# Attention in a fused block: P.V. runs that stop at the accumulator's copy, transposes of maxima joined to them, a sixth buffer of exponentials, and divisions forced behind a unit

## The chip, the cores and the metric

One NeuronCore of a Trainium2 chip runs the whole program. The metric is device time in microseconds (us) of one execution. TensorE is called PE here, VectorE DVE, ScalarE ACT, GpSimd POOL and the DMA-issuing SyncE SP, as in the profile.

## What is computed

A transformer block on 2048 tokens of 576 numbers: sliding-window attention (32 heads of 18, a window of 256 keys), and beside it a gated branch whose spatial product is a 2048 x 2048 matrix; both work on the same normed input.

```python
qkv = (x @ wqkv).reshape(B, S, 3, H, Dh).transpose(2, 0, 3, 1, 4)
scores = einsum("bhqd,bhkd->bhqk", q, k) * Dh ** -0.5
mask = (idx[:, None] - idx[None, :] >= 0) & (idx[:, None] - idx[None, :] < 256)
p = softmax(where(mask, scores, -1e9))
s = einsum("bhqk,bhkd->bhqd", p, v).transpose(...).reshape(B, S, D) @ wo
...
z = gelu(x @ w_in); z1 = z[:Fh]; z2 = layernorm(z[Fh:])
g = silu((z1 * (w_sp @ z2 + b_sp)) @ w_out)
return x_in + s * g
```

## The kernel before

The program goes through stages one after the other: projections to q, k, v and the second half of z (to 430 us of the profile), attention (442 to 892 us), the output projection `wo` (892 to 954 us), the spatial product (`acc`, to about 1655 us) and the last product (`c`). Only the order inside attention changes.

**Attention is cut into 16 units**: 4 heads times half of the tokens (1024 queries); units 0 to 7 have the first half, 8 to 15 the second. Of a unit PE does five kinds of work:

- *maxima* (M, L600): a score block with queries on the partitions, `sp`, 3 PSUM banks; DVE reduces it to a maximum per query (L604). 32 for a unit. When all are there, DVE makes the negative maxima (L613, L614), PE *transposes* them (T, L623), DVE copies them out (L626) and four DMAs put them into two extra rows of q (L630), so that the next product already has the maximum taken off.
- *scores* (S, L724): keys on the partitions, `tps`, 2 PSUM banks; ACT takes the exponential into a buffer `pt` (L728), one `pt` for four heads and one block of 128 keys, and POOL masks its two edges (L736, L739). `PTB` is the number of `pt` buffers, 5.
- *P.V.* (V, L752): four matmuls, one for each head and each of 32 columns, add one key block to up to 512 queries of the accumulator `ops`, of which there is one. A column of 128 queries of this, four heads together, is called a block below; the program has 360. When 512 queries are done, ACT copies the accumulator out (L767). The sums of the exponentials are in it as one more row.
- *fills* (L671): the first half of z, w_in's product for z1, which nothing in attention needs; 1944 matmuls of 512 columns in two streams, `ma` and `mb`, whose results ACT copies out (L676) and SP stores.

M, S and fills use 64 of the array's rows each, so that two streams run at once, one on each half of the rows; P.V. and T use all 128 rows. A change from the one to the other is called a switch here, and what stands between two of them a run or a region.

**After the second copy of a unit** `finish` queues the division: SP loads the sums (L814), DVE inverts them (L787), SP writes them out (L789) and reads them back four times, spread over partitions, into `rp` (L794, one buffer), POOL divides in four parts (L798), SP stores the result to `o_d` (L803). For the last unit the same is written after the loop (L810, L807, L808, L794, L798, L803).

**The order is written by a planner in the kernel**: it keeps a clock of its own with fixed costs, and emits at each step what its clock allows: a P.V. run if `pv_now` says so, else a score or a maximum, else a fill. `waiting` holds actions with a due time (loads, stores, divisions), which `tick` emits when the clock has passed it. All engines then execute in exactly the emitted order, each its own queue, SP's DMAs too. `GUARD` (150 ns) is the planner's margin for a finished operand. When nothing is left in the queues, the remaining `waiting` actions are emitted in order of time. Then follow 448 matmuls of `wo` (L1157), for 8 tiles of 256 tokens, two steps of 128 tokens each; each tile's operand is loaded from `o_d` (L978, L980), split by ACT (L1143) and DVE (L1144), and its result copied by ACT into one of two `so` buffers (L1190) that SP stores (L1192). Tiles 4 to 7 need the last unit.

Of the kernel before, what the change touches and what calls it, by code (L numbers as in the profile page):

```python
# [39 lines left out]
RMN = 16  # L40
QR = 5
STEPS = 27
GUARD = 150
# [6 lines left out]
DIVIDE_AT = (20000, 21200, 22400, 23600, 26500, 27000, 27500, 28000)  # L50
WARM = 54
SPB = 3
PTB = 5


ET = mybir.EngineType
# [8 lines left out]
def kernel(  # L65
# [170 lines left out]
    with ExitStack() as early:  # L236
# [283 lines left out]
        with ExitStack() as ph:  # L520
# [33 lines left out]
            waiting = []  # L554
            clock = 0.0
# [8 lines left out]
            def use(engine, ns, drain=0):  # L564

                busy[engine] = max(busy[engine], clock + 200) + ns
                return busy[engine] + drain

            def tick():
                for w in list(waiting):  # L570
                    if w[0] <= clock:
                        waiting.remove(w)
                        w[1]()
# [11 lines left out]
            maxima = {}  # L585
# [109 lines left out]
            def load_v(u):  # L695
# [3 lines left out]
                sp.dma_start(vg[:, :kn], v_d[k0:k0 + kn, :, g * 4 * VW:g * 4 * VW + 89].rearrange("s p c -> p s c"))  # L699
                vgs[u] = vg  # L700

            vgs, pts, left, o_ps, ous, last, todo, later = {}, {}, {}, {}, {}, [], [], []

            def steps_of(half):
# [37 lines left out]
            def pv(u, kb, qa, qz):  # L742
                g, half = UNITS[u]
                pt = pts[u, kb]
                k0 = 0 if half == 0 else 6
                c = qa // 4
                first = max(4 * c - 2, 0)
                if kb == first:
                    o_ps[c] = ops.tile([P, 512], F32, name="ops")
                hi = min(4 * c + 3, qz)  # L750
                for j in range(4):
                    pe.matmul(o_ps[c][32 * j:32 * j + 32, (qa - 4 * c) * P:(hi - 4 * c + 1) * P],  # L752
                              vgs[u][:, kb - k0, j * VW:j * VW + 32], pt[:, j, (qa - kb) * P:(hi - kb + 1) * P],
                              start=kb == first, stop=kb == 4 * c + 3, skip_group_check=True)
                spend_both((hi - qa + 1) * 218)
                if hi == qz:
                    pts.pop((u, kb))
                else:
                    later.append([0.0, u, kb, hi + 1, qz])
                if kb == 4 * c + 3:  # L760
                    if c % 2 == 0:
                        while parts.get(u - 2):
                            part(u - 2)
                        ous[u] = (ap_.tile([P, HS], F32, name="ou", bufs=2) if u < NU - 1 else
                                  tail()[:, 0:HS])
                    ou = ous[u]
                    act.activation(ou[:, c % 2 * 512:c % 2 * 512 + 512], o_ps.pop(c), AF.Copy)  # L767
                    free_at = use("act", 500, 120)
                    for t in later:
                        t[0] = free_at  # L770
                    if c % 2 == 1:
                        finish(u, ou)

            parts = {}

            def part(u):
                if parts[u]:
                    parts[u].pop(0)()

            def finish(u, ou):  # L780

                g, half = UNITS[u]
                cs = slice(half * HS, half * HS + HS)
                den = aa.tile([P, HS // 32], F32, name="den")
                rp = ap_.tile([P, HS], F32, name="rp", bufs=1) if u < NU - 1 else f32(slots[4][:, 0:HS])
                def invert():
                    dve.reciprocal(den, den)  # L787
                    t = use("dve", 270) - clock + 300
                    after(t + (1500 if u < NU - 2 else 300), lambda: sp.dma_start(r_d[u].rearrange("h (a b) -> (h a) b", b=HS // 32), den))  # L789
                    for i in range(4):  # L790
                        after(t + (FETCH_AT if u < NU - 2 else 4500) + 400 * i, partial(sums, i))

                def sums(i):
                    sp.dma_start(rp[32 * i:32 * i + 32, :], r_d[u][i:i + 1, :].to_broadcast([32, HS]))  # L794

                def divide(a, n=4):
                    hs = slice(a * HS // n, (a + 1) * HS // n)
                    pool.tensor_tensor(ou[:, hs], ou[:, hs], rp[:, hs], ALU.mult)  # L798
                    use("pool", 2900 / n)

                def store(i):
                    h = 4 * g + i
                    sp.dma_start(o_d[h * DH:(h + 1) * DH, cs], ou[32 * i:32 * i + DH, :])  # L803

                if u == NU - 1:
                    def put_last():
                        dve.reciprocal(den, den)  # L807
                        sp.dma_start(r_d[u].rearrange("h (a b) -> (h a) b", b=HS // 32), den)  # L808

                    last.extend([lambda: sp.dma_start(den, ou[DH::32, :]), put_last,  # L810
                                 lambda: [sums(i) for i in range(4)], lambda: [divide(a, 2) for a in range(2)],
                                 lambda: [store(i) for i in range(4)]])
                else:
                    after(busy["act"] - clock + 1000, lambda: sp.dma_start(den, ou[DH::32, :]))  # L814
                    sooner = 10000 if u == NU - 2 else 0
                    after(max(INVERT_AT - sooner, 4500), invert)
                    parts[u] = [partial(divide, a) for a in range(4)] + [partial(store, i) for i in range(4)]
                    for ns in DIVIDE_AT:
                        after(ns - sooner + (3500 if sooner else 0), partial(part, u))
# [183 lines left out]
            with ExitStack() as heads:  # L1003
# [41 lines left out]
                taken, max_done = {0: 2 * RMN}, {0: max_split(0)}  # L1045

                def pv_now():
                    n = next((i for i, t in enumerate(todo) if t[0] + GUARD > clock), len(todo))
                    if n >= 2 or (n and not score_queue[0] and not score_queue[1]):
                        size = sum(t[4] - t[3] + 1 for t in todo[:n])  # L1050
                        return n if size >= 9 or len(pts) >= PTB or not score_queue[0] else 0
                    return 0

                def pv_run(n):

                    spend_both(110)
                    for v in [v for v in maxima if taken.get(v) == 2 * RMN and max_done[v] <= clock]:
                        max_end(v)
                        ended.add(v)
                    for _ in range(n):  # L1060
                        pv(*todo.pop(0)[1:])
                        if later and later[0][0]:
                            todo[:0] = later
                            later.clear()
                            break
                    spend_both(220)

                while score_queue[0] or score_queue[1] or todo or filling:
# [3 lines left out]
                    while opened < NU and all(not q or q[0][0] >= opened for q in score_queue):  # L1072
                        open_unit(opened)
                        opened += 1
                    full = [v for v in maxima if taken.get(v) == 2 * RMN and max_done[v] + GUARD <= clock]
                    n = pv_now()
                    if n or full:
                        pv_run(n)
# [609 lines left out]
```

## Time and profile before

| | us |
|---|---|
| median of three runs | 1862.79 |
| the three runs | 1862.79, 1864.56, 1860.42 |
| the profiled execution | 1859.38 |
| its span, first to last instruction | 1857.3 |
| first score of attention | 442.05 |
| last P.V. run begins | 885.49 |
| first matmul of `wo` | 891.87 |

The profiled execution is 3.4 us below the median of the runs. Times in the profile are counted from the span's start. A timeline row gives start, duration, engine, source line, operation, output and inputs, and the count of merged instructions; in brackets stands the idle time of the engine before it and what ended it. A matmul's duration is its latency: consecutive ones overlap, so that the distance between starts tells what one costs. P.V. matmuls leave two records each (1408 for 704). Of the 512 maxima 468 have a record inside attention's window, the rest being missing or earlier.

### The profile page before, as it was taken

What the parts mean: (1) busy time and instruction counts of PE and PEld (TensorE: products, weight loads), DVE (VectorE), ACT (ScalarE), POOL (GpSimd) and SP (SyncE); (2) the same over time, 40 slices, a digit from 0 to 9 for tenths busy, and PEclk for the clock granted to TensorE, in tenths of its full rate; (3) what the DMA queues carried; (4) which work ended last, traced back from release to release, by engine and by line L of the source; (5) the groups of instructions that cost most, each with busy time, mean ns of one, the idle gap of its engine ahead of it and who ended that gap; (6) DMA issues with size and microseconds to landing.
All of it is one profiled execution on the core that took longest, in us unless ns stands there. A gap on an engine that the chain in (4) does not pass through costs nothing.

```text
span 1857.3 us, 38172 instructions
## 1 busy us (share of the span) xinstructions
PE 1823.3 (98%) x14363; PEld 1590.3 (86%) x14363; DVE 1138.2 (61%) x2289; ACT 947.8 (51%) x1758; POOL 430.7 (23%) x507
## 2 busy tenths in 40 slices
PE   8999999999999999999999999999999999999998
PEld 8999999997777777776898878888888888899998
DVE  6321333467766677771246788667876567758876
ACT  5433322225666576667467566465554544444443
POOL 3332333334465455556100000111100000000000
PEclk9999999999999999999999999999999999999999
DMA  8885688887566666754776777789777656786554
GB/s 254 206 229 169 232 278 281 290 258 224 154 194 168 187 174 179 189 161 142 239 266 225 236 239 244 258 293 302 252 262 234 185 183 198 250 266 187 160 159 134
DMA packets 266920, 405.75 MB, mean 218 GB/s; under 512 B 52336, under 2 KB 180592, under 8 KB 266608
## 3 DMA queue, kind: packets, MB, share of 16 engines
q1 hardware_dynamic: 266736, 403.32, 70.4%
q8 instruction: 113, 1.85, 0.4%
q14 instruction: 71, 0.58, 0.1%
HBM read 285.35 MB, written 117.09 MB: 217 GB/s over the span
## 4 chain that ended last, share of the span: by engine, by line
PE 82%; DVE 7%; DMA 5%; SPq 2%; ACT 2%; issue 2%; POOL 0%; DVEq 0%; ACTq 0%; POOLq 0%
PE acc L1431 34%; PE mb L206 11%; PE c L1522 7%; PE ma L671 6%; PE mb L671 5%; PE ma L206 5%; PE ops L752 4%; PE tps L724 3%; PE sp L600 3%; PE wops L1157 2%; SPq L363 1%; DMA st_d<-qkhl 1%; DVE junk L604 1%; DVE spl L116 1%; PE ma L380 0%
## 5 line engine op out<-in xcount | busy, mean ns | idle before, releaser
L1431 PE MATMUL acc<-spl,zh 128*128 128x512 f32 x1008 | 392.6, 390 | 1.1 <-DVE spl L116 0.9
L1431 PE MATMUL acc<-sph,zh 128*128 128x512 f32 x1008 | 392.2, 389 | 0.0
L1431 PE MATMUL acc<-sph,zl 128*128 128x512 f32 x1008 | 392.1, 389 | 0.0
L604 DVE CUSTOM_DVE_ANT_0 junk<-sp,band 128x384 bf16<-128x384 f32 (+1 forms) x512 | 276.4, 540 | 114.9 <-PE sp L600 33.6
L728 ACT ACTIVATE pt<-tps 128x384 f32<-128x384 f32 (+2 forms) x576 | 231.2, 441 | 121.6 <-PE tps L724 78.0
L116 DVE TENSOR_TENSOR spl<-spr,sph 128x1024 fp32r<-128x1024 f32 x168 | 210.2, 1251 | 40.0 <-ACT sph L115 39.3
L671 PE MATMUL mb<-b,z1wh 64*128 64x512 f32 x648 | 225.2, 400 | 2.5 <-ACT z1o L676 2.1
L671 PE MATMUL ma<-b,z1wh 64*128 64x512 f32 x648 | 224.8, 399 | 0.6 <-ACT zt L948 0.4
L1431 PEld LDWEIGHTS acc<-spl,zh 128*128 128x128 f32 x1008 | 189.2, 188 | 41.7 <-DVE spl L116 2.8
L1431 PEld LDWEIGHTS acc<-sph,zh 128*128 128x128 f32 x1008 | 189.3, 188 | 39.3
L1431 PEld LDWEIGHTS acc<-sph,zl 128*128 128x128 f32 x1008 | 189.3, 188 | 39.3
L115 ACT ACTIVATE zh<-b 128x384 fp32r<-128x384 f32 x168 | 87.3, 520 | 211.1 <-PE acc L1431 206.7
L115 ACT ACTIVATE sph<-spr 128x1024 fp32r<-128x1024 f32 x168 | 176.0, 1048 | 14.5 <-DMA spr<-in_w_sp_dram 5.3
L724 PE MATMUL tps<-att 56*128 56x384 f32 (+1 forms) x576 | 177.2, 345 | 2.2 <-ACT pt L728 1.2
L116 DVE TENSOR_TENSOR zl<-b,zh 128x384 fp32r<-128x384 f32 x168 | 99.6, 593 | 124.0 <-ACT zh L115 123.9
L600 PE MATMUL sp<-att 54*128 54x384 f32 (+1 forms) x512 | 161.2, 349 | 2.0 <-DVE mx L604 1.8
L1522 PE MATMUL c<-b,o 128*128 128x288 f32 x1056 | 143.3, 295 | 0.5 <-DVE o L116 0.5
L1522 PEld LDWEIGHTS c<-b,o 128*128 128x128 f32 x1056 | 141.0, 188 | 0.8 <-DVE o L116 0.7
L949 DVE BATCH_NORM_STATS2 st<-zt 128x6 f32<-128x384 f32 x96 | 49.3, 548 | 132.1 <-ACT zt L948 132.0
L671 PE MATMUL ma<-b,z1wl 64*128 64x512 f32 x324 | 128.4, 396 | 0.0
L671 PE MATMUL mb<-b,z1wl 64*128 64x512 f32 x324 | 127.8, 394 | 0.0
L724 PEld LDWEIGHTS tps<-att 56*128 56x128 f32 x576 | 99.7, 184 | 30.5 <-issue 9.5
(219 smaller groups left out, 4189.6 us busy)
## 6 DMA issues: line engine op xcount, KB each, us to landing
spr<-sc_d SPq DMA_DIRECT2D x96, 512.0 KB
spr<-in_w_sp_dram SPq DMA_DIRECT2D x72, 512.0 KB
zr<-z_d SPq DMA_DIRECT2D x144, 192.0 KB
z_d<-zt SPq DMA_DIRECT2D x48, 384.0 KB
z_d<-z1o SPq DMA_DIRECT2D x72, 256.0 KB
z1t<-z_d SPq DMA_DIRECT2D x72, 256.0 KB
y_d<-z1t SPq DMA_DIRECT2D x72, 256.0 KB
a<-in_w_sp_dram SPq DMA_DIRECT2D x64, 256.0 KB
```

The costliest lines, as they stand in the source:

```text
L115: act.activation(hi, src, AF.Copy)
L116: dve.tensor_tensor(lo, src, f32(hi), ALU.subtract)
L206: pe.matmul(banks[h][:, :n], *both[h][i], start=i == 0, stop=i == STEPS - 1)
L600: pe.matmul(ps[:, :w], q_of(u, j)[0:54, i * P:(i + 1) * P], k_of(u, j)[0:54, k0:k0 + w], start=True, stop=True)
L604: dve.tensor_tensor_reduce(out=junk[:, :w], in0=ps[:, :w], in1=band[:, m0:m0 + w], scale=1.0, scalar=-3.0e38, op0=ALU.add, op1=ALU.max, ac ...
L671: pe.matmul(ps, w, x_, start=n == 0, stop=n == STEPS - 1)
L724: pe.matmul(ps[:, :m * P], k_of(u, j)[:, (kb - base) * P:(kb - base + 1) * P], q_of(u, j)[:, (a - lo) * P:(a - lo + m) * P], start=True, s ...
L728: act.activation(pt[:, j, d0:d0 + n * P], ps[:, (qa - a) * P:(qa - a + n) * P], AF.Exp, scale=scale)
L752: pe.matmul(o_ps[c][32 * j:32 * j + 32, (qa - 4 * c) * P:(hi - 4 * c + 1) * P], vgs[u][:, kb - k0, j * VW:j * VW + 32], pt[:, j, (qa - kb) ...
L949: dve.bn_stats(st2[:, s, pc, :], zv)
L1431: pe.matmul(acc[j], z[:, ps], w[:, cs], start=s == i == 0 and n in OPENS, stop=s == 7 and i == 2, skip_group_check=True)
L1522: pe.matmul(banks[key][:, :288], y, w, start=begin and k == n == 0, stop=close and k == 8 and n == 2, skip_group_check=True)
```

## The change

Six edits, all in the planner:

1. `pv_run` also stops a run when the accumulator has been given to ACT's copy (`if not o_ps: break`), and `pv_now` allows no new run before that copy is done on the planner's clock (`ops_free`). Before, a run stopped at a copy only if key blocks were left over that also belong to the next 512 queries.
2. A P.V. run needs 12 blocks instead of 9 (unless buffers are full or no score is left).
3. A unit's maxima are transposed only 1000 ns (`LATE`) after the planner's end of their negation; and, apart from a P.V. run that happens anyway, only when the score queue's ninth entry (`DUE` = 8) belongs to that unit.
4. `PTB` is 6.
5. `finish` of a unit first emits what is left of the four divisions of the unit before.
6. `tick` goes through its actions in order of due time.

```diff
-PTB = 5
+LATE = 1000
+DUE = 8
+PTB = 6
...
-                for w in list(waiting):
+                for w in sorted(waiting, key=lambda w: w[0]):
...
+            ops_free = [0.0]
...
                     free_at = use("act", 500, 120)
+                    ops_free[0] = free_at
...
                 cs = slice(half * HS, half * HS + HS)
+                while len(parts.get(u - 1, ())) > 4:
+                    part(u - 1)
...
                 def pv_now():
+                    if not o_ps and ops_free[0] + GUARD > clock:
+                        return 0
...
-                        return n if size >= 9 or len(pts) >= PTB or not score_queue[0] else 0
+                        return n if size >= 12 or len(pts) >= PTB or not score_queue[0] else 0
...
+                def max_due(v):
+                    queue = score_queue[0]
+                    return not queue or queue[min(DUE, len(queue) - 1)][0] >= v
...
-                    for v in [v for v in maxima if taken.get(v) == 2 * RMN and max_done[v] <= clock]:
+                    for v in [v for v in maxima if taken.get(v) == 2 * RMN and max_done[v] + LATE <= clock]:
...
                             break
+                        if not o_ps:
+                            break
...
-                    full = [v for v in maxima if taken.get(v) == 2 * RMN and max_done[v] + GUARD <= clock]
+                    full = [v for v in maxima if taken.get(v) == 2 * RMN and max_done[v] + LATE <= clock
+                            and max_due(v)]
```

The number of instructions of each kind on PE stays the same: 704 P.V. matmuls, 576 scores, 512 maxima, 16 transposes, 1944 fills. What changes is how they stand:

| PE, attention | before | changed |
|---|---|---|
| runs of P.V. | 71 | 56 |
| transposes alone, between two regions | 12 | 7 |
| transposes at the head of a P.V. run | 4 | 9 |
| switches (stretches of full rows) | 83 | 63 |
| runs that go on behind an accumulator's copy | 4 | 0 |
| fills behind the last P.V. | 48 | 0 |

PE, the end of one unit and the begin of the next (units 11 and 12); `ops` is the accumulator, a new number is a new accumulator, `pt` the exponentials. Before:

```order
L724 MATMUL tps_13029<-att0_2227 128x384
L752 MATMUL ops_12825<-pt_12849,vg_12021 32x128 x4
L752 MATMUL ops_13039<-pt_12895,vg_12540 32x128 x4
L752 MATMUL ops_13039<-pt_12935,vg_12540 32x256 x4
L724 MATMUL tps_13050<-att0_2227 128x384
L600 MATMUL sp_13055<-att3_6847 128x384
```

and with the change, where the line numbers are 2 or 3 higher:

```order
L727 MATMUL tps_13104<-att0_2227 128x384
L755 MATMUL ops_12926<-pt_12852,vg_12075 32x256 x4
L755 MATMUL ops_12926<-pt_12908,vg_12075 32x128 x4
L602 MATMUL sp_13125<-att3_6847 128x384
L727 MATMUL tps_13129<-att0_2227 128x384
...
L625 MATMUL sp_13221<-ident_70,ms_13141 64x128
L755 MATMUL ops_13225<-pt_12974,vg_12607 32x128 x4
L755 MATMUL ops_13225<-pt_13016,vg_12607 32x256 x4
L755 MATMUL ops_13225<-pt_13056,vg_12607 32x384 x4
L755 MATMUL ops_13225<-pt_13103,vg_12607 32x384 x4
```

The run that went on from one accumulator into the next is cut at the copy, and the next accumulator's run comes 38 rows later, with four key blocks and a transpose (L625) at its head.

PE, the end of attention. Before, from the last run but one:

```order
L752 MATMUL ops_14676<-pt_14634,vg_14047 32x384 x4
L752 MATMUL ops_14676<-pt_14672,vg_14047 32x256 x4
L671 MATMUL ma_14747<-b0_92,z1wh_14254 128x512
L671 MATMUL mb_14732<-b0_92,z1wl_14255 128x512
L671 MATMUL ma_14747<-b3_95,z1wh_14254 128x512
L671 MATMUL mb_14732<-b0_92,z1wh_14254 128x512
L752 MATMUL ops_14676<-pt_14712,vg_14047 32x128 x4
L671 MATMUL ma_14747<-b0_92,z1wl_14255 128x512
...
```

and with the change, from the last score before the last three runs:

```order
L727 MATMUL tps_14757<-att0_2227 128x256
L755 MATMUL ops_14635<-pt_14590,vg_14152 32x256 x4
L755 MATMUL ops_14635<-pt_14631,vg_14152 32x128 x4
L727 MATMUL tps_14769<-att0_2227 128x256
L727 MATMUL tps_14772<-att1_2228 128x256
L755 MATMUL ops_14776<-pt_14590,vg_14152 32x128 x4
...
L755 MATMUL ops_14776<-pt_14739,vg_14152 32x256 x4
L727 MATMUL tps_14799<-att1_2228 128x256
L755 MATMUL ops_14776<-pt_14756,vg_14152 32x128 x4
L1172 MATMUL wops_14868<-att2_2229,ohl0_14855 128x288 x2
```

The last fill now stands eight rows ahead of the first of these, with seven scores between them, and `wo` comes right behind the last P.V., where 48 fills stood.

POOL, the same place, with the change (`pt_14756` is the last key block's exponentials, `ou_14405` the result of unit 14):

```order
L739 AFFINE_SELECT pt_14711<-pt_14711 128x4x128
L742 AFFINE_SELECT pt_14711<-pt_14711 128x4x128
L739 AFFINE_SELECT pt_14739<-pt_14739 128x4x128
L804 TENSOR_TENSOR ou_14405<-ou_14405,rp_14600 128x256 x3
L739 AFFINE_SELECT pt_14756<-pt_14756 128x4x128
L804 TENSOR_TENSOR ou_14405<-ou_14405,rp_14600 128x256
L804 TENSOR_TENSOR att5_14473<-att5_14473,att4_6849 128x512 x2
```

Three divisions of unit 14 stand ahead of the last mask; before, all four stood ahead of the last four masks. On SP the store of unit 14's result (L809) moves from ahead of the last fills' stores to the row just ahead of the load of the last unit's sums (L816).

## Prediction

> **What bounds the kernel now.** First the page, then the stretches of 25 us through attention.
>
> ```profile
> PE 1823.3 (98%) x14363; PEld 1590.3 (86%) x14363; DVE 1138.2 (61%) x2289; ACT 947.8 (51%) x1758; POOL 430.7 (23%) x507
> PE 82%; DVE 7%; DMA 5%; SPq 2%; ACT 2%; issue 2%; POOL 0%; DVEq 0%; ACTq 0%; POOLq 0%
> ```
>
> ```profile
> core 0: us, PE busy (x) PEld busy (x) DVE busy (x) ACT busy (x) POOL busy (x), PEclk, DMA share, GB/s
> 625.00:650.00 25.00, 23.06 (x196) 18.12 (x198) 16.46 (x59) 11.59 (x26) 8.85 (x15) 0.93 0.65 169
> 675.00:700.00 25.00, 25.00 (x271) 19.52 (x265) 18.10 (x64) 17.97 (x46) 14.91 (x23) 1.00 0.73 203
> 900.00:925.00 25.00, 23.65 (x176) 23.19 (x175) 7.46 (x7) 11.01 (x17) 3.61 (x2) 1.00 0.79 247
> ```
>
> PE carries 82% of the chain that ended last, and in attention it is covered nearly everywhere: 25.00 of 25 us in an ordinary stretch, with DVE and ACT at 18. But a busy PE here is latency laid end to end; what one switch, wait or fill costs is seen only between starts. So attention is bound by PE's in-order queue: fills, which wait for nothing, fill it up while scores and maxima wait for ACT and DVE.
>
> At the end something else binds:
>
> ```profile
> 885.49 0.43 PE L752 MATMUL ops<-pt,vg 128*32 128x128 f32 x8
> 891.55 0.39 PE L671 MATMUL ma<-b,z1wl 64*128 64x512 f32 x1
> 891.87 22.66 PE L1157 MATMUL wops<-att,ohl 128*128 128x288 f32 x168
> 915.40 0.78 PE L1157 MATMUL wops<-att,ohl 128*128 128x288 f32 x4 [0.87 <-ACT ohl L1143]
> 916.66 37.04 PE L1157 MATMUL wops<-att,ohl 128*128 128x288 f32 x276 [0.48 <-DVE ohl L1144]
> ```
>
> ```profile
> 885.99 0.60 ACT L767 ACTIVATE att<-ops 128x512 f32<-128x512 f32 x1 [1.91 <-PE ops L752]
> 888.00 0.62 SPq L810 DMA_DIRECT2D den<-att  x1
> 896.90 4.57 DMA att<-r_d
> 901.69 3.62 POOL att L798 x2
> 905.32 1.37 SPq L803 DMA_DIRECT2D o_d<-att  x4
> 910.56 2.90 DMA s_d<-so
> 914.09 1.27 ACT ohl L1143
> ```
>
> The chain of waits goes from the last unit's copy over its sums, their inverse, the division and its store (SP stands at L803 until POOL is done at 905.3); behind this in SP's queue is the store of `so`, for which ACT's queue stands before it can split the operand of the fourth token tile. PE reaches that tile with only 0.87 + 0.48 us to wait, and is then continuous for 37 us. So the time of everything behind is the last P.V. plus 916.66 - 885.49 = 31.2 us, whatever PE does meanwhile. **The question is when the last P.V. comes.** The 48 fills behind it merely fill that latency.
>
> **Switches: -6.6 us.** A run of eight blocks, and one of one block:
>
> ```profile
> 785.40 0.39 PE L671 MATMUL mb<-b,z1wh 64*128 64x512 f32 x1
> 785.72 1.93 PE L752 MATMUL ops<-pt,vg 128*32 128x384 f32 x24
> 787.58 0.44 PE L600 MATMUL sp<-att 54*128 54x384 f32 x1
> ...
> 459.22 0.38 PE L724 MATMUL tps<-att 56*128 56x256 f32 x1
> 459.53 0.43 PE L752 MATMUL ops<-pt,vg 128*32 128x128 f32 x8
> 459.89 0.44 PE L600 MATMUL sp<-att 54*128 54x384 f32 x1
> ```
>
> From the last start before to the first behind it is 2.18 us with eight blocks and 0.67 with one: 0.22 for a block, and 0.45 without any. In those 0.45 a half-array matmul would have run anyway: fills follow each other at 0.12 us (48 stand between 885.49 and 891.55 above, in some 5.7). That leaves 0.33 us for a switch, in both directions together. There are 83 before and 63 after: 20 x 0.33 = 6.6. The blocks, 360, stay.
>
> **Waits for the copy within a run: -3.7.** The four runs that went on behind a copy look like this:
>
> ```profile
> 664.14 0.33 PE L724 MATMUL tps<-att 56*128 56x384 f32 x1
> 664.41 0.86 PE L752 MATMUL ops<-pt,vg 128*32 128x256 f32 x16
> 666.03 0.43 PE L752 MATMUL ops<-pt,vg 128*32 128x128 f32 x8 [0.76 <-POOL ou L798]
> 666.38 0.50 PE L671 MATMUL ma<-b,z1wh 64*128 64x512 f32 x1
> ```
>
> Four blocks in 2.24 us where 0.45 + 4 x 0.22 = 1.33 would do: 0.91, and 4 x 0.91 = 3.7. The profile names POOL, but the releaser is ACT's copy between the two accumulators (L767 stands elsewhere as the releaser of L752). The change cuts all four runs there; scores, maxima and fills stand in the gap.
>
> **Transposes: -2.9.** They stood 150 ns of planner time behind DVE's negation, and DVE is later than planned:
>
> ```profile
> L623 PE MATMUL sp<-ident,ms 128*64 128x128 f32 x15 | 4.5, 299 | 2.9 <-DVE ms L614 2.9
> ```
>
> 2.9 us of idle PE. With 1000 ns, and a place in front of a P.V. run for 9 of 16, this should go. What is late next is q's two extra rows, which the unit's scores need: between a transpose and its unit's first score stand about as many PE instructions as before (in the first half a few more, in the second the same), so I put nothing there; the bound is the 0.7 us that L724 waits for `att<-mhl` now, doubled.
>
> **The fills that stood behind the last P.V.: +5.7.** They come before it now, 48 x 0.12. This takes back most of the switches: PE saves time, but spends it on fills that were hidden in the latency at the end.
>
> **An end without fills: +4.8.** From the last fill to the last P.V. PE now has only what ACT and POOL let it have:
>
> ```profile
> 877.28 1.51 ACT L728 ACTIVATE pt<-tps 128x384 f32<-128x384 f32 x3
> 880.90 0.66 ACT L728 ACTIVATE pt<-tps 128x256 f32<-128x256 f32 x2 [1.42 <-PE tps L724]
> 884.21 0.63 POOL L736 TENSOR_SCALAR_AFFINE_SELECT pt<-pt 128x512 f32<-128x512 f32 x1 [1.31 <-ACT pt L728]
> ```
>
> Eight scores, paced by two `tps` banks (score 0.34, exponential 0.5 or 0.38, two in flight: 0.35 to 0.45 each), and one split among them, 4.2 us; a P.V. run of three blocks 0.9; ACT's copy 0.6 and its hand-over 0.1; the next accumulator's run of eleven blocks 2.5; then the last score 0.35, its exponential 0.3, its mask 0.7, the last block 0.4: 10.0 us. PE's work in it is 15 blocks (3.3), eleven scores (0.9), three switches (1.0): 5.2. So 4.8 us of PE are lost. Bounds: 2.5, if the scores' exponentials have run ahead under the fills; 7, if the last mask is held up (below).
>
> **Smaller terms.** The load of the last unit's sums was issued 1.4 us behind the end of the copy (886.59 to 888.00), since SP issued two tiles' loads of `o_d` first; now those stand earlier, but four stores of unit 14 stand just ahead of it, 1.4 us of issue: -0.3, bounds -1.4 and +1. The 12-block rule, the sixth buffer and the sorted actions change the order only, and are in the counts. A stall at 640 us has no cause in the order alone:
>
> ```profile
> 633.32 7.21 DMA z_d<-z1o
> 641.28 0.49 PE L671 MATMUL mb<-b,z1wh 64*128 64x512 f32 x1 [1.54 <-ACT z1o L676]
> 643.16 0.62 PE L671 MATMUL mb<-b,z1wl 64*128 64x512 f32 x1
> 640.00:645.00 5.00, 3.72 (x20) 3.36 (x22) 2.54 (x10) 3.96 (x10) 2.00 (x3) 0.72 0.64 177
> ```
>
> A store of a fill's result took 7.2 us, ACT's copy waited for its buffer, PE for ACT, 1.54 us; then the granted clock was 0.72 over 5 us (1.4 us lost, fills at 0.62 instead of 0.39). Where SP's queue is interleaved otherwise this may go or stay, 0 to -2.9; I take -1.5. The same dip can come in the new idle time at the end: with `wo` right behind the last P.V., PE waits for copy and split of the first tile (0.60 + 1.26 + 1.23, by ACT and DVE behind 885.99) and later some 3.5 us at the fourth tile. The first is covered by the chain; behind the second PE is what binds. 0 to 1.4 by the row above; +0.7.
>
> [...]
>
> **Sum.** -6.6 - 3.7 - 2.9 + 5.7 + 4.8 - 0.3 - 1.5 + 0.7 = -3.8 us. On the profiled 1859.4 that is 1855.6; the runs' median lies 3.4 above that execution, and 1862.8 - 3.8 = 1859.0. About 0.2%, 3.7 us, is what a measurement of this kernel can tell from no change; the forecast stands on that line.
>
> **Rivals.**
>
> *No gain*: the freed PE time is all spent on the end. Fills (5.7), the empty end at its bound (7) and the dip (1.4) are 14.1 against 13.2 from switches, copies and transposes: 1863.7, give or take 1.5. For it: the end is bound by latency, not by PE. Against: 7 needs the mask held up too.
>
> *Slower: the restart behind longer runs.* During P.V., ACT has two `tps` banks to work off, 0.5 us each (877.28: three in 1.51), then stands still; now runs of four key blocks, some 2.5 us, are the common ones. The time in which ACT stands is the same P.V. time less 1.0 us for each of 71 runs before, and for each of 56 now: 15 us more of it in all. Had ACT no slack, attention would be 15 longer and the time 1862.8 - 3.8 + 15 = 1874. It has (17.97 of 25 us busy above), but in the last two units fills are few. From half of these 15 on the change is slower by 0.2%; a little over that, 1868, is its likeliest size.
>
> *The mask behind the divisions* belongs with it in sign: POOL's last mask stands behind three divisions of unit 14, which need the reread sums.
>
> ```profile
> 857.05 0.60 ACT L767 ACTIVATE ou<-ops 128x512 f32<-128x512 f32 x1 [0.98 <-PE ops L752]
> 874.63 1.42 POOL L798 TENSOR_TENSOR ou<-ou,rp 128x256 f32<-128x256 f32 x2 [1.00 <-DMA rp<-r_d]
> ```
>
> Now it is 17.0 us from the copy's end to the first division. The order gives about 8 us of PE work from unit 14's last P.V. to the last fill, and 9 to the last mask: 17. Three divisions are 2.2 us, so that the last P.V. would be late by about as much: 1861.2, in the second bound above.
>
> *More than forecast*: the end loses only 2.5, the load of sums comes right behind the copy (-1.4), the stall at 640 us is gone whole (-2.9), no dip: -3.8 - 2.3 - 1.1 - 1.4 - 0.7 = -9.3, 1853.5.
>
> *The change doesn't do what it says*: the order shows that it does; no chance.
>
> **How the numbers follow.** Forecast, 0.48, 1856 to 1862 by itself, a little over half of it beyond the line (0.27); no gain, the mask's 1861.2 included, 0.18; slower 0.16; more than forecast 0.18. Faster by over 0.2%: 0.27 + 0.18 = 0.45; within: 0.21 + 0.18 = 0.39; slower: 0.16. The range reaches from the large gain to the edge of the slower case, 1853 to 1866.5, and leaves out most of that one and the tail of the gain.
>
> **What would show it.** Right: L767 no longer a releaser of L752 on PE; L623's wait for L614 near 0; 63 switches at 0.33; the last P.V. between 880 and 884 us, and `wo`'s long group 31 us behind it, with 3 us of idle PE ahead of it. Wrong: a wait of L752 for POOL L804 at the last block (divisions), idle PE between scores with L731 as releaser through units 8 to 15 (restart), or the last P.V. later than 886 us.

## Result and the profile after

| | before | changed |
|---|---|---|
| median of the runs shown together, us | 1862.63 | 1905.85 |
| the four runs | 1860.42 to 1864.56 | 1902.45 to 1909.69 |
| ratio (95% interval) | | 1.0232 (1.0207 to 1.0257) |
| profiled execution; its span | 1859.38; 1857.3 | 1905.45; 1903.6 |
| last P.V. run begins | 885.49 | 932.50 |

The change costs 43 us; the forecast was 1859.0. All of it is lost in attention: the span grew by 46.3 us, the last P.V. comes 47.0 later. Two lines of the changed kernel's page, engine shares and the chain that ended last:

```profile
PE 1844.1 (97%) x14363; PEld 1611.2 (85%) x14363; DVE 1138.4 (60%) x2289; ACT 949.5 (50%) x1758; POOL 429.2 (23%) x507
PE 78%; DMA 9%; DVE 6%; SPq 3%; ACT 2%; issue 2%; POOL 1%; DVEq 0%; ACTq 0%; POOLq 0%
```

PE is busy for 21 us more with the same 14363 instructions, and carries less of the chain; DMA has 9% instead of 5. One row for attention, from the first score to the last P.V., shows what the longer time is made of (columns: stretch, its length, busy time of PE, PEld, DVE, ACT, POOL, granted clock, DMA share, GB/s). Before, then changed:

```profile
442.00:885.50 443.50, 431.82 (x4272) 328.52 (x4273) 281.60 (x1001) 295.72 (x729) 237.36 (x350) 1.00 0.63 174
```

```profile
443.90:932.50 488.60, 455.29 (x4309) 350.33 (x4310) 278.52 (x999) 298.42 (x731) 234.48 (x348) 0.95 0.58 159
```

Of the 45.1 us, 21.6 are idle PE (443.50 - 431.82 = 11.7 before, 488.60 - 455.29 = 33.3 now) and 23.5 are longer busy time. Of the latter the 48 fills that moved ahead of the last P.V. are 5.7 at the price of the prediction. The other 17.8 fit the clock: in the trace's clock records PE runs at 0.50 for 44.4 us of this stretch, 3.4 before, and half of the 41.0 more would be 20.5. **Nearly half is waiting, and most of the rest is the clock behind the waiting.** The largest stall, on PE, and the clock around it:

```profile
548.22 0.39 PE L673 MATMUL ma<-b,z1wl 64*128 64x512 f32 x1
554.24 0.68 PE L727 MATMUL tps<-att 56*128 56x384 f32 x1 [5.63 <-ACT pt L731]
```

```profile
546.00:552.00 6.00, 1.75 (x12) 0.94 (x11) 1.96 (x8) 0.00 (x0) 3.03 (x4) 0.99 0.70 194
552.00:558.00 6.00, 3.76 (x20) 3.76 (x22) 1.40 (x5) 3.16 (x8) 1.53 (x3) 0.50 0.26 84
558.00:564.00 6.00, 6.00 (x67) 4.71 (x66) 3.04 (x11) 3.33 (x10) 1.93 (x3) 0.94 0.49 117
```

PE stands for 5.63 us for an exponential; when it goes on, the granted clock is 0.50 and the matmuls take 0.62 instead of 0.39. The exponential is late because ACT stands at a copy of the accumulator:

```profile
543.61 0.56 ACT L688 ACTIVATE z1wh<-z1raw 128x384 fp32r<-128x384 f32 x1
553.21 0.60 ACT L770 ACTIVATE ou<-ops 128x512 f32<-128x512 f32 x1 [9.05 <-DMA z_d<-z1o]
```

The profile names a store of a fill's result, which this copy has nothing to do with. Its output `ou` has two buffers, so unit 3 writes where unit 1's result is still being stored; SP and POOL show that store and its division:

```profile
543.61 0.27 SPq L809 DMA_DIRECT2D o_d<-ou  x1
...
549.19 0.31 SPq L809 DMA_DIRECT2D o_d<-ou  x1
```

```profile
540.77 2.81 POOL L804 TENSOR_TENSOR ou<-ou,rp 128x256 f32<-128x256 f32 x4 [4.25 <-DMA rp<-r_d]
```

POOL waited 4.25 us for the reread inverses, SP for POOL, ACT for the stores. There used to be more time. Unit 1's second copy, then before the change that copy, the unit's last store, and unit 3's first copy:

```profile
516.15 0.60 ACT L770 ACTIVATE ou<-ops 128x512 f32<-128x512 f32 x1 [0.92 <-PE ops L755]
```

```profile
502.65 0.60 ACT L767 ACTIVATE ou<-ops 128x512 f32<-128x512 f32 x1 [0.91 <-PE ops L752]
...
534.69 0.32 SPq L803 DMA_DIRECT2D o_d<-ou  x1
...
541.47 0.60 ACT L767 ACTIVATE ou<-ops 128x512 f32<-128x512 f32 x1
```

The last store is issued some 33 us behind the second copy in both (549.19 - 516.15 = 33.0 now, 32.0 before). But ACT reaches the copy of the unit after next 28.0 us behind it now (553.21 - 9.05 = 544.16), where 38.8 us lay between before. The second stall of this kind came about otherwise, on the side of the store: unit 4's copy is reached 38.9 us behind unit 2's, but unit 2's last store is issued 40.2 us behind, since POOL begins the unit's divisions 30.0 us behind its copy instead of 22.0.

```profile
576.73 0.33 SPq L809 DMA_DIRECT2D o_d<-ou  x1
581.52 0.60 ACT L770 ACTIVATE ou<-ops 128x512 f32<-128x512 f32 x1 [6.04 <-DMA o_d<-ou]
```

The other family of stalls is on DVE. Its queue, and SP's, at PE's stall of 3.8 us at 824:

```profile
821.39 0.28 DVE L628 COPY mhl<-sp 64x128 f32<-64x128 f32 x1
827.28 0.35 DVE L793 RECIPROCAL den<-den 128x32 f32<-128x32 f32 x1 [5.62 <-DMA den<-ou]
827.55 0.50 DVE L606 CUSTOM_DVE_ANT_0 junk<-sp,band 128x384 bf16<-128x384 f32 x1
```

```profile
818.71 0.47 SPq L642 DMA_DIRECT2D z1raw<-in_w_z_dram  x1
820.23 0.28 SPq L809 DMA_DIRECT2D o_d<-ou  x1
...
821.85 0.62 SPq L820 DMA_DIRECT2D den<-ou  x1
```

The load of the sums was issued behind a weight of 576 KB and the stores of the unit before; the reciprocal stands 5.62 us for it, the next maximum (L606) stands behind the reciprocal, and PE waits for a free `sp` bank. Over the program, from the waits of the changed kernel (us in total, times, longest):

```profile
DVE den L793 <- DMA den<-ou: 23.5, 9, 5.6
...
PE tps L727 <- ACT pt L731: 14.6, 9, 5.6
...
PE sp L602 <- DVE mx L606: 9.7, 9, 3.8
...
ACT ou L770 <- DMA o_d<-ou: 6.0, 1, 6.0
```

### The profile page after: what moved, and what is told of

The parts are those of the page before. It is cut to its first block, busy times and chain, and to the rows that moved or that the text cites. A ratio compares the mean times of both kernels' runs of the same rounds, so it can differ in the third digit from the quotient of the medians.

```text
span 1903.6 us, 38155 instructions
## 1 busy us (share of the span) xinstructions
PE 1844.1 (97%) x14363; PEld 1611.2 (85%) x14363; DVE 1138.4 (60%) x2289; ACT 949.5 (50%) x1758; POOL 429.2 (23%) x507
## 4 chain that ended last, share of the span: by engine, by line
PE 78%; DMA 9%; DVE 6%; SPq 3%; ACT 2%; issue 2%; POOL 1%; DVEq 0%; ACTq 0%; POOLq 0%
PE acc L1446 34%; PE mb L208 10%; PE c L1537 7%; PE ma L208 6%; PE ma L673 5%; PE mb L673 5%; PE ops L755 4%; PE tps L727 2%; PE sp L602 2%; PE wops L1172 2%; SPq L365 1%; DMA den<-ou 1%; DMA att<-st_d 1%; DMA st_d<-qkhl 1%; DVE junk L606 1%
## 5 line engine op out<-in xcount | busy, mean ns | idle before, releaser
L606 DVE CUSTOM_DVE_ANT_0 junk<-sp,band 128x384 bf16<-128x384 f32 (+1 forms) x512 | 275.8, 539 | 143.9 <-PE sp L602 55.4
L673 PE MATMUL mb<-b,z1wh 64*128 64x512 f32 x648 | 229.9, 410 | 3.5 <-ACT z1o L678 3.2
L673 PE MATMUL ma<-b,z1wh 64*128 64x512 f32 x648 | 230.9, 410 | 0.5 <-ACT zt L954 0.4
L727 PE MATMUL tps<-att 56*128 56x384 f32 (+1 forms) x576 | 182.3, 351 | 16.0 <-ACT pt L731 14.6
L727 PEld LDWEIGHTS tps<-att 56*128 56x128 f32 x576 | 104.4, 190 | 48.0 <-ACT pt L731 23.0
L739 POOL TENSOR_SCALAR_AFFINE_SELECT pt<-pt 128x512 f32<-128x512 f32 x128 | 81.4, 636 | 216.5 <-ACT pt L731 209.5
```

The source lines that it names most:

```text
L606: dve.tensor_tensor_reduce(out=junk[:, :w], in0=ps[:, :w], in1=band[:, m0:m0 + w], scale=1.0, scalar=-3.0e38, op0=ALU.add, op1=ALU.max, ac ...
L673: pe.matmul(ps, w, x_, start=n == 0, stop=n == STEPS - 1)
L727: pe.matmul(ps[:, :m * P], k_of(u, j)[:, (kb - base) * P:(kb - base + 1) * P], q_of(u, j)[:, (a - lo) * P:(a - lo + m) * P], start=True, s ...
L739: pool.affine_select(out=pt[:, :, 0:P], in_=pt[:, :, 0:P], pattern=[[0, 4], [1, P]], compare_op=ALU.is_ge, fill=0.0, base=0, channel_multi ...
```

## Experiments

Theory Q: the new order brings copies, sums and stores nearer to each other; ACT, DVE and SP stand at the head of their in-order queues; PE idles, and pays again at half clock. Rival L: long P.V. runs starve ACT. Rival R: the loss lies in the other edits, not in the sixth buffer. Rival D: the forced divisions are the cause. Times are medians; each ratio is to the kernel before, run on the same chip beside it. "Idle" is the length of attention less PE's busy time, one profiled execution each.

| run | us | ratio (95%) | attention | PE busy | idle | clock |
|---|---|---|---|---|---|---|
| five_buffers | 1877.49 | 1.0087 (1.0066 to 1.0107) | 456.6 | 437.4 | 19.2 | 0.98 |
| before_six | 1897.07 | 1.0190 (1.0166 to 1.0214) | 480.8 | 448.5 | 32.3 | 0.97 |
| no_forced_divisions | 1895.31 | 1.0183 (1.0155 to 1.0212) | 476.3 | 449.0 | 27.3 | 0.96 |
| third_ou | 1892.17 | 1.0168 (1.0153 to 1.0183) | 476.4 | 450.8 | 25.6 | 0.96 |
| ou_late_recip | 1881.20 | 1.0101 (1.0075 to 1.0127) | 466.0 | 443.3 | 22.7 | 0.98 |
| five_ou_late_recip | 1866.87 | 1.0021 (1.0006 to 1.0037) | 444.3 | 433.4 | 10.9 | 0.99 |
| before_ou_late_recip | 1858.96 | 0.9983 (0.9969 to 0.9997) | 447.6 | 434.9 | 12.7 | 0.99 |
| before_z1o | 1855.95 | 0.9964 (0.9950 to 0.9977) | 440.3 | 431.9 | 8.4 | 1.00 |

**Which edit.** One part is taken back, or made alone.

```diff
-PTB = 6
+PTB = 5
```

> The whole change, but with five exponential buffers instead of six. Theory Q (the loss is 25 us of idle PE in some fifteen stalls, each followed by half-clock periods; the stalls are ACT, DVE and SP standing at the head of their queues, because units end at less even distances and the first copy of a unit follows the end of the unit before by about half the former time): with five buffers the runs are short again, the first copy moves away from the unit before, and most stalls go: 1860 to 1880 us. Rival R (the loss comes from what the other four edits do, whatever the number of buffers): 1890 to 1910.

1877.5: 28 of the 43 us are the sixth buffer's. What is left is of the same kind; one copy of an accumulator stands 5.4 us.

```diff
-PTB = 5
+PTB = 6
```

> The kernel before with a sixth exponential buffer and nothing else of the change. Theory Q, by which the sixth buffer makes units end unevenly and brings the copies close behind the unit before: 1878 to 1900 us. Rival R: within 5 us of the kernel before, 1856 to 1866.

1897.1, 35 us above the kernel before, by this one line. Rival R falls as the main cause. The 35 us of the sixth buffer alone and the 16 of all the rest (five_buffers) are more than 43, so the two do not simply add. Here other queues stand too: ACT's copies stand 5.07 us once for `ou`, but also 4.12 and 4.03 us for a fill's buffer `z1o`, and PE's longest stall is P.V. waiting for a mask that stands on POOL behind a division, for whose operands POOL stood 12.41 us:

```profile
605.45 0.72 POOL L798 TENSOR_TENSOR ou<-ou,rp 128x256 f32<-128x256 f32 x1 [12.41 <-DMA att<-st_d]
606.13 0.64 POOL L736 TENSOR_SCALAR_AFFINE_SELECT pt<-pt 128x512 f32<-128x512 f32 x1
606.72 0.64 POOL L739 TENSOR_SCALAR_AFFINE_SELECT pt<-pt 128x512 f32<-128x512 f32 x1
```

```profile
608.19 1.51 PE L752 MATMUL ops<-pt,vg 128*32 128x384 f32 x8 [5.16 <-POOL pt L739]
```

The cures below were not tried on this kernel.

```diff
-                while len(parts.get(u - 1, ())) > 4:
-                    part(u - 1)
```

> The changed kernel without the forced divisions; six buffers and all else kept. Theory Q: the sixth buffer decides, and the first copies of the early units still follow close on the unit before, so the long waits for the copied accumulator near 550 and 580 us stay: 1885 to 1905 us. Rival D (the forced divisions, which put stores into SP's order sooner than POOL can divide, are the cause): at most 1875.

1895.3, and its copies wait 10.7 us in two places for `o_d<-ou`. Rival D falls as the main cause; the ratio is 0.0049 below that of the whole change, each known to 0.003, so some 9 us may be this edit's.

**The copies.** A third buffer, the order of every engine unchanged:

```diff
-                        ous[u] = (ap_.tile([P, HS], F32, name="ou", bufs=2) if u < NU - 1 else
+                        ous[u] = (ap_.tile([P, HS], F32, name="ou", bufs=3) if u < NU - 1 else
...
```

> The changed kernel with a third buffer for the copied accumulator, and nothing else: the order of every engine stays, and the computation too. Theory Q: the two copies at 548 and 578 us no longer stand for 9.05 and 6.04 us, the PE gaps of 6.0 and 4.2 us go with their half-clock periods of 6.8 and 10.2 us: 15 to 20 us less, 1886 to 1891 us. Rival L (long runs starve ACT of scores, and the gaps are the restart): unchanged, 1902 to 1908.

13.7 us less (12 by the ratios), a little short of the range. In the waits for the copy only P.V. itself is left:

```profile
DVE den L793 <- DMA den<-ou: 26.6, 10, 7.5
...
ACT ou L770 <- PE ops L755: 22.7, 23, 2.8
```

So the copies did wait for their output buffer, where the profile named other transfers. The runs are as long as before: rival L falls for these stalls. But DVE now stands 7.5 us once, up to 817, where the longest was 5.6: a relieved queue meets the next late load.

**The reciprocal.** First its load was moved from SP to ACT:

```diff
-                    after(busy["act"] - clock + 1000, lambda: sp.dma_start(den, ou[DH::32, :]))
+                    after(busy["act"] - clock + 1000, lambda: act.dma_start(den, ou[DH::32, :]))
```

> The changed kernel with the load of the sums issued by ACT behind the copy instead of by SP. Theory Q: the reciprocal on DVE no longer waits for it (23.5 us over 9 times), so the maxima behind it are in time; the gaps at 738, 795, 824 and 858 us (2.0, 1.1, 4.1, 1.4) and one half-clock period go: 8 to 13 us less, 1892 to 1898 us. If the transfer itself is late, not its place in SP's queue, or ACT then waits instead: unchanged, 1902 to 1910.

1902.79, ratio 1.0224 (1.0207 to 1.0242): a miss. DVE's waits for the load fell from 23.5 to 6.9 us, its gaps went, but PE's idle time did not: ACT, on which PE waits for exponentials, now also issues 15 loads of 0.55 us, and the stores of `ou` still hold two of its copies for 10.7 us. PE's waits for exponentials rose from 14.6 to 19.9 us. With the third buffer added:

> Both: the third buffer for the copied accumulator and the load of the sums issued by ACT. Theory Q: the two gains add, 23 to 33 us less than the changed kernel, 1872 to 1883 us. Rival L: 1902 to 1908.

1896.26, 1.0190 (1.0171 to 1.0209): no better than the third buffer alone (1.0168, 1.0153 to 1.0183). The load moved the wait from DVE's queue to ACT's. Then the reciprocal itself was moved to a later place in DVE's order instead:

```diff
-                    dve.reciprocal(den, den)
                     t = use("dve", 270) - clock + 300
+                    after(hold, lambda: dve.reciprocal(den, den))
-                    after(t + (1500 if u < NU - 2 else 300), lambda: ...
+                    after(t + (hold + 1500 if u < NU - 2 else 300), lambda: ...
```

(`hold` is 3000, 0 for the last two units.)

> The changed kernel with a third buffer for the copied accumulator and the reciprocal put 3 us later into DVE's order (its store likewise; every other order stays). Against the run with the third buffer alone (1892.2). Theory Q: the maxima no longer wait behind a reciprocal whose load has not landed; the gaps at 812 (6.0), 658, 670 and 694 us shrink, with one half-clock period of 6.8 us: 8 to 13 us less, 1879 to 1884 us. If the maxima are late for another reason: 1890 to 1894.

1881.2, 11 us less than with the third buffer alone; DVE's waits for the sums, 26.6 us there, are 0.8 us now. The two cures together take 25 of the 43 us back without a change in PE's order. With five buffers as well:

> Five exponential buffers, the third buffer for the copied accumulator and the later reciprocal, all other edits of the change kept. Theory Q: of the 20 us in gaps over 1 us with five buffers, those behind the reciprocal (495, 615, 652, 769, 825 us: 9.5 us) and behind the copy (621 us: 5.5) go, with 10 us at half clock: 1858 to 1866 us, level with the kernel before. Rival R (the other four edits cost time of themselves): 1870 to 1878.

1866.9, 0.21% above the kernel before (0.06 to 0.37). With both cures the sixth buffer costs 14 us (1881.2 against 1866.9), where it costs 28 without them. And the same cures on the kernel before:

> The kernel before with the third buffer for the copied accumulator and the later reciprocal. Its own gaps over 1 us sum to 9.4 us and one half-clock period of 3.4 us, of which the one behind the negations at 465 us and the one behind a copy at 589 us could go: 0 to 4 us less, 1856 to 1862 us by theory Q. By rival L unchanged.

0.17% faster, just measurably (its profiled execution, in the table, was its slowest, 1864.51). What SP and the fills' copies still held up was tried on the changed kernel with the two cures: `z1o` with three buffers, and the stores of `o_d` issued by POOL.

```diff
-                    sp.dma_start(o_d[h * DH:(h + 1) * DH, cs], ou[32 * i:32 * i + DH, :])
+                    (sp if u == NU - 1 else pool).dma_start(o_d[h * DH:(h + 1) * DH, cs], ou[32 * i:32 * i + DH, :])
```

> The changed kernel with the third buffer for the copied accumulator, the later reciprocal, a third z1o buffer, and the stores of o issued by POOL behind its own divisions instead of by SP (28.9 us of SP's waits for POOL). Plan and PE order as in the changed kernel. Theory Q: the gaps at 507 (z1o, 3.1), 617 (3.1), 682 and 692 us (1.7 and 6.4, loads of q and k late on SP) go with 17 us at half clock: 12 to 20 us less than 1881.2, 1861 to 1869 us. If the loads are late because the DMA queue is full, not because SP stands: 1874 to 1882.

1875.76, 1.0077 (1.0054 to 1.0100): a miss, within the range of the other reading, that the loads are late because the DMA queue is full. That reading stays open. What the profile shows is that SP no longer waits for POOL, and that POOL, which issues the stores itself, holds the masks instead: P.V. waits 6.0 us for them in all, 2.3 with the two cures alone. One place on POOL:

```profile
538.50 2.83 POOL L805 TENSOR_TENSOR ou<-ou,rp 128x256 f32<-128x256 f32 x4 [5.91 <-DMA att<-st_d]
541.62 0.54 POOL L810 DMA_DIRECT2D o_d<-ou  x1 [0.29 <-POOL ou L805]
542.17 0.65 POOL L739 TENSOR_SCALAR_AFFINE_SELECT pt<-pt 128x512 f32<-128x512 f32 x1
```

**The clock.** In the kernel before, TensorE transposes a tile ahead of one P.V. run in each of units 9 to 14, DVE copies it and passes over it k times, TensorE waits for the last pass.

```diff
+                    pe.transpose(ps[:, :P], ident, ident)
...
+                    dve.tensor_copy(pl, ps[:, :P])
+                    for _ in range(k):
+                        dve.tensor_scalar(pl, pl, 1.0, None, ALU.mult)
...
+                    pe.transpose(ps[:, :P], pl, ident)
```

> The kernel before with a planted stall in six units of the second half (units 9 to 14, ahead of one P.V. run each): TensorE transposes a tile, DVE copies it and goes over it once more, TensorE transposes the copy and waits for it. The stall is about 0.5 us of hand-over and two DVE passes of at most 0.28 us (the copy of 64x128): some 1 us. Theory C (an idle PE costs again by half-clock periods, but only from some 1.5 us on): no further half-clock period, at most 6 x 1 = 6 us, 1862 to 1869 us. Rival (any gap is followed by one): 6 x 1.7 more.

> The same six stalls with six DVE passes behind the copy: 1.3 to 2.5 us each. Theory C: most of the six are followed by 3.4 us at half clock, so each costs its idle time and up to 1.7 us more: 8 to 25 us, 1871 to 1888 us. Rival (an idle PE costs its idle time alone): the clock stays at 1.0 behind them, 8 to 15 us.

> The same with sixteen passes: 3 to 5 us each. Theory C: each of the six is followed by one or two half-clock periods of 3.4 us, 18 to 30 us idle and 10 to 20 us of lost clock: 1891 to 1913 us, with 20 to 41 us of half clock in the six units. Rival: 18 to 30 us and the clock at 1.0.

| run | us | ratio (95%) | us for each stall | planted gaps in the profile | half-clock periods behind them |
|---|---|---|---|---|---|
| stall_1 | 1871.60 | 1.0054 (1.0037 to 1.0071) | 1.7 | 0.65 to 1.4 | 3.4 once |
| stall_6 | 1889.42 | 1.0156 (1.0128 to 1.0184) | 4.7 | 1.95 to 3.42 | 3.4 at four of six |
| stall_16 | 1910.95 | 1.0266 (1.0247 to 1.0284) | 8.3 | 4.57 to 6.03 | 6.8 at five, 10.2 at one |

The profiled execution of stall_6 was its fastest, 1877.65, 3.0 us above the one before for each stall, with gaps of 2.5 us on average. The stalls of 16 passes, five us each, cost 8.3. With 6 passes, the third and fourth rows being the second stall:

```profile
697.80:701.60 3.80, 0.39 (x3) 0.14 (x2) 3.39 (x11) 0.01 (x1) 2.62 (x3) 1.00 0.61 166
701.60:706.60 5.00, 5.00 (x32) 4.05 (x36) 2.55 (x9) 2.38 (x6) 1.59 (x3) 0.66 0.13 32
737.80:740.80 3.00, 0.36 (x3) 0.17 (x2) 2.55 (x11) 0.55 (x2) 1.22 (x2) 1.00 0.07 16
740.80:744.20 3.40, 3.40 (x29) 2.08 (x33) 1.13 (x4) 1.85 (x4) 0.00 (x0) 0.50 0.00 0
```

In these rows the clock is full while PE stands, and half soon after it starts again, for 3.4 us. Here an idle stretch cost again behind its end, 8.3 us for some five; the rival that it costs its idle time alone falls. That stall_1 took 10 us, not 6 at most, is a miss. It has no more half clock than the kernel before (3.4 us in attention), but 6.3 us more of idle PE and 4.8 of busy PE, part of which are the planted transposes. The same planted instructions with 16 passes have 24.1 us more of idle PE than stall_1 and 14.5 of busy PE (451.1 against 436.6), with 54.6 us at half clock instead of 3.4. So a us at half clock cost 0.28 us here (14.5 of 54.6 - 3.4), not the half that one would reckon from a granted clock of 0.50.

**The terms on PE.** On the kernel before with both cures (1858.96, 0.9983) the parts of the change that were to save PE time were made singly.

> The kernel before with the third buffer for the copied accumulator and the later reciprocal (1859.0), plus the part of the change by which a P.V. run stops at the copy and waits for the accumulator (with the forced divisions and the sorted actions, which move next to nothing with five buffers). The term of the prediction for waits within a run was -3.7 us. Theory Q (the terms on PE hold where no queue stands): 1853 to 1858 us. If the planner only cuts the runs elsewhere and pays the switches again: 1858 to 1863.

1864.13, 0.9995 (0.9979 to 1.0012).

> The same base (1859.0) plus only the rule by which transposes of maxima wait for a P.V. run or a due time. The prediction's term was -2.9 us. Theory Q: 1854 to 1858 us. If the later maxima hold back the scores of the next unit: 1860 to 1868.

1859.41, 0.9980 (0.9968 to 0.9992).

> Both of these on the same base: the change without the sixth buffer and the size of 12, with the two cures. The terms add to -6.6 us by the prediction: 1850 to 1857 us by theory Q; at 1859 or above the terms on PE do not reach the time.

1870.15, 1.0037 (1.0023 to 1.0050). Neither of the first two can be told from its base by the intervals, which are too wide to show a gain of 2 us, and both together are slower. In that profile PE waits 1.98 and 2.66 us for late exponentials at 516 and 860, in the latter case because ACT stands 3.02 us for a load of `z1raw`; singly, neither kernel has these two stalls.

**The end.** The last 12 fill steps of each row kept until the row's last scores are issued:

```diff
-                        if filling and bank_free[r] <= clock and fill(r):
+                        if filling and bank_free[r] <= clock and (
+                                not score_queue[0] or total - z1_done[r] > 12) and fill(r):
```

> The changed kernel with the third buffer and the later reciprocal (1881.2), with the last 12 fill steps of each row kept until the last scores of that row are issued. PE order is the same up to the last unit. In that base the last unit shows 1.5 us before the last P.V., some 1.5 us between scores, and 6.8 us at half clock (902.4, 912.6). Theory: fills cover these waits and the dips go: 3 to 7 us less, 1874 to 1878 us. If the fills only move the idle time forward: 1880 to 1883.

1886.79, 1.0120 (1.0099 to 1.0141), a miss. Kept back, the fills are missing a few us earlier, where PE now stands between scores, up to 1.0 us at a time; 10.2 us at half clock begin at 895.

**The version that beats both** is the kernel before with both cures and a third buffer for `z1o`; PE's order is not touched.

> The kernel before with the third buffer for the copied accumulator, the later reciprocal and a third z1o buffer; its order is that of before_ou_late_recip (1859.0), whose z1o waits at 622 and 646 us (2.05 and 1.25) and 3.4 us of half clock then go: 2 to 5 us less, 1854 to 1857 us. If the z1o copy is late for another reason: 1857 to 1861.

1855.95, 0.36% below the kernel before (0.23 to 0.50) and about 2.6% below the changed one.

## Why the prediction was wrong

**The step that failed** is "The 12-block rule, the sixth buffer and the sorted actions change the order only, and are in the counts". The sixth buffer alone costs 35 us. It saves switches by letting key blocks pile up for longer runs, and so moves the points at which units end. The forecast counted what that moves on PE and kept everything else as fast as it was, except at the end and at 640 us. But the output buffers, the one accumulator and the in-order queues of ACT, DVE, POOL and SP turned over with little to spare: with 38.8 us from a copy to the next use of its buffer nothing waited, with 28.0 the copy stood 9.05 us, and where a division came 8 us later, 38.9 were too few. The 12-block rule of that sentence costs nothing with five buffers: five_ou_late_recip (1866.87, 1.0021) has it, and stop_and_joined (1870.15, 1.0037) is the same kernel without it. The sorted actions were not run alone.

- *Switches, -6.6, and waits for the copy, -3.7.* As an order they came: 63 stretches of full rows, and no P.V. waits for a copy within a run. As time, the copies' 3.7 did not: stop_at_copy gains nothing on its base. The switches were not tried by themselves. Counted in the traces from the first score on, which leaves out one transpose, every kernel with five buffers has 80 to 83 such stretches and every one with six 62 to 70, so the switches saved are the sixth buffer's, and no run has them without its waits. Whether a switch is worth 0.33 us stays open.
- *Transposes, -2.9.* PE's idle time ahead of them fell from 2.9 to 0.5 us. In time, joined_transposes gains nothing over its base that can be told; its interval does not exclude 2.9.
- *Fills from behind the last P.V., +5.7.* They moved, as the prediction had it.
- *An end without fills, +4.8.* Right in kind, mis-sized. From the last fill to the last P.V. were 10.0 us booked. The changed kernel:

```profile
919.45 0.39 PE L673 MATMUL ma<-b,z1wl 64*128 64x512 f32 x1
...
922.87 1.28 PE L727 MATMUL tps<-att 56*128 56x256 f32 x3 [0.15 <-ACT pt L731]
924.08 1.51 PE L755 MATMUL ops<-pt,vg 128*32 128x256 f32 x16
...
926.31 4.75 PE L755 MATMUL ops<-pt,vg 128*32 128x128 f32 x40 [0.20 <-ACT att L770]
930.98 0.38 PE L727 MATMUL tps<-att 56*128 56x256 f32 x1
932.50 0.43 PE L755 MATMUL ops<-pt,vg 128*32 128x128 f32 x8 [1.14 <-POOL pt L739]
```

 13.1 us, and 2.3 of the 3.1 more are in one row: the accumulator's last long run, booked at 2.5, took 4.75. The clock is at 0.50 for 6.8 us from 923.9 on, although no wait of PE in the 10 us ahead of it is over 0.51 us. What brought this period on, no run shows.
- *Load of the last sums, -0.3, and the 31.2 us behind the last P.V.* 961.83 - 932.50 = 29.3: about two us better, of the right order.
- *Stall at 640 us, -1.5.* It went from there, and its kind came back at 508, where PE stood 2.7 us for a fill's copy, and larger on ACT and DVE. One stall was priced as one stall, not as a sign that a queue had no slack.
- *Clock dip, +0.7.* 17.8 us by the busy time, 20.5 if half of the 41.0 us more at half clock is lost. It was booked once, at the end, after the one dip in attention before: 3.4 us at 0.50, behind a wait of 1.54 us. In attention of the changed kernel the clock records have eight such periods, four of 3.4 us, three of 6.8 and one of 10.2. Six of them began during a wait of PE of 2.04 to 5.63 us or within 1.3 us of its end, the first during one of 0.97, the last behind waits of at most 0.51; a wait of 1.67 us that ended at 740.4 had none behind it. In this study's profiles 23 of 29 stalls of 2 to 3 us were followed by one.
- *Rivals.* "The restart behind longer runs" gave the sign, and idle PE between scores, released by exponentials, did appear, 14.6 us. But it had named units 8 to 15, and these have 1.4 us of it. Its mechanism was not the cause: the third buffer took the two largest of these waits away with runs as long as ever. "The mask behind the divisions" did not decide: 1.14 us at the last block. "No gain" and "more than forecast" stayed on PE, like the forecast.
- *What would show it wrong* named three signs. P.V. never waited for a division at the last block, and exponentials were hardly waited for in units 8 to 15; the last P.V. later than 886 us came, at 932.5.

What stays open: with six buffers and every queue cure, 1875.8 is still 14 us above the kernel before. Its profile has the same kind of stalls in other places (18.9 us idle, 27 at half clock). So the mechanism is shown for the 25 us that the two cures took back, and read from the profiles for the rest; no order was found in which six buffers are free of it.

## What to carry to other kernels

A kernel whose engines run in an order written by hand has slack that no busy share shows: before a change moves where units end, list for each rotated buffer and for each load ahead of a reciprocal, a mask or a copy how long it had, and how long it has in the new order. Price a stall of more than 2 us on TensorE, as an estimate from these runs, as its idle time plus a quarter to a half of the 3.4 us or more at half clock that came behind 50 of 56 such stalls here (0.28 in the planted stalls, 0.43 in the changed kernel: 17.8 of 41.0 us). Give the buffers behind the queues one more turn first (`ou`, `z1o`, and a reciprocal behind its load: 0.36% here); shorter PE sequences pay only once nothing stands.

## What the runs showed of the hardware

Over the 20 profiled executions of this study PE's gaps in attention were followed by a half-clock period in 12 of 124 cases of 0.65 to 1.25 us, 4 of 16 of 1.25 to 1.5, 7 of 14 of 1.5 to 2, 23 of 29 of 2 to 3, and in all 27 above 3 us. The same gap of 1.95 us had one in one unit of stall_6 and none in another. In the profiles of the kernel before and of the changed one alone it is 1 of 2 of 1.5 to 2 us, 2 of 2 of 2 to 3, and 4 of 4 above 3. These are counts of what followed, and they show no sharp threshold: three of the five planted gaps of 1.95 to 2.74 us in stall_6 were followed by one, and a period also came at the end of the changed kernel's attention, at 923.9, behind waits of at most 0.51 us. And a wait that the profile puts down to one transfer (9.05 us, "z_d<-z1o") was another's: a third buffer for `ou` removed it.
